# Whole rows for two slabs of W1, the ragged unit and a value tile around the key folds, and the second layer two token tiles ahead, in a gated mix of linear attention and a ReLU layer

## The chip, the cores and the metric

The kernel runs on one core of a Trainium2 chip. The metric is the device time of one execution in microseconds (us). Profiles are of one execution each. TensorE (PE in the profile, PEld for its weight loads), VectorE (DVE), ScalarE (ACT), GpSimd (POOL) and SyncE (SP) run side by side, and each works through its own queue in order. TensorE writes its results into PSUM, which has eight banks of 128 x 512 fp32.

## The reference

The input x has 2048 tokens of width 512. All data are bf16. A linear attention with 32 heads and a two-layer ReLU network read the same x, and a gate per token mixes them:

```python
q, k, v = split(x @ wqkv)                    # 32 heads of 16
pq, pk = q @ w_phi[h], k @ w_phi[h]          # per head, 16 x 16
phi_q = concat(softmax(pq), softmax(-pq))    # 32 features per head
phi_k = concat(softmax(pk), softmax(-pk))
kv, z = phi_k^T v, sum over s of phi_k       # per head
o = (phi_q kv) / (phi_q z + 1e-6)
a = o @ wo
b = relu(x @ w1) @ w2                        # 512 -> 1376 -> 512
g = sigmoid(sum(x * gate_w))
out = g * a + (1 - g) * b
```

## The kernel before

TensorE's work is cut by token tiles of 128 (16 of them, m = 0 to 15) and by chunks of 512 tokens (4 of them, c). The program is written out by hand: each call appends instructions to the queues of the engines, with named events to wait for. The order of the calls is the order on every engine. A list `free` holds, for each PSUM bank, the event that frees it; whoever takes the bank next waits for that event as the list has it at that point of the program.

Loads (L165 to L189) are issued by SP, in this order: the first 512 tokens of x, W1 in slabs of 128 rows (`loadw1`, L161; slab 0 in two pieces, slabs 1 to 3 with the first 1024 of 1376 columns), between slabs 2 and 3 a DMA transpose of part of x (event x0t, L175), then the remaining 352 columns of all four slabs (event w1r, L178), w_phi, the value weights, the query and key weights through two DMA transposes (wqk0, wqk1, L185), and the other three chunks of x through DMA transposes (L188).

Start on TensorE: `slab(t)` (L518) multiplies slab t with the first 512 tokens, for eight blocks of 128 hidden columns, into eight banks. Slab 2 needs x0t. Two more blocks (`hunit(0, 8)` and `hunit(0, 9)`, L269) need all of W1. `hunit(c, k)` computes hidden block k of chunk c with four matmuls, and ScalarE (or VectorE) writes its ReLU to HT. The last 96 hidden columns and the gate's column are the ragged unit `rest(c)` (L279): 16 small matmuls, two activations on ScalarE and a DMA transpose from SP. `pre(i)` (L300) folds w_phi into the query weights (i = 0 to 3, wqk0) and the key weights (i = 4 to 7, wqk1), four matmuls each; the result goes from PSUM to WQK by VectorE (even i) or ScalarE (odd i). `vtile(m)` (L401) computes the values of tile m with four matmuls into bank 2.

Middle: for each tile, `atile(m)` (L319) computes the query and key scores with eight matmuls and starts the softmax chain on ScalarE, VectorE and GpSimd; `kv(m - 3)` (L417) adds the tile's keys and values into banks 6 and 7; then come `vtile(m + 3)` and one to three units of the list `mid` (L563). A pair (c, k) of that list is `hunit(c, k)`, and k = -1 is `rest(c)`. The units left over (`late`, L566) follow, among them the last `kv` calls and `kvfin`, with which VectorE completes the sums. `qchain` (L380) is the query half of the softmax chain; that of tile 15 is called at the end.

Output loop (L608): `nd(m)` (L454) multiplies the query features with the sums (eight short matmuls), VectorE takes the reciprocal (L464) and multiplies (L468), and SP transposes the tile to OT by DMA. `finB(m, bank)` (L479) is the second layer of the ReLU network for a token tile: 11 matmuls into one bank. `finA(m, bank)` (L490) is the output projection: four matmuls, after which ScalarE scales by the gate (L497). `comb(m)` (L502) then adds (1 - g) times the bank of `finB` on VectorE (L506), which frees that bank, and issues the store. `finB` takes the banks of `FB = (4, 5, 7)` by tile modulo 3. In the loop `finB` runs one tile ahead of `finA`. Tile 15 is computed in two column parts in banks 4 and 3 at the end.

Of the kernel before, what the change touches and what calls it, by code (L numbers as in the profile page):

```python
# [68 lines left out]
def bass_gated_mix__linear_kernel_hedgehog__dense_activation_relu__prompt_kernel(  # L69
# [16 lines left out]
    DFF = B_w1.shape[1]  # L86
    P = 128
    NT = S // P
# [13 lines left out]
    KU = KT - 1  # L102
    NR = DFF - KU * P

    with ExitStack() as es:
# [8 lines left out]
        W1 = E(nc.sbuf_tensor("W1", [P, NDT, DFF + 8], BF16))  # L114
# [36 lines left out]
        p = _Plan(["sp", "pool", "act", "dve", "pe"])  # L151
# [9 lines left out]
        def loadw1(t, c0=0, c1=DFF, tag=""):  # L161
            p.dma("sp", lambda e: e.dma_start(  # L162
                out=W1[:, t, c0:c1], in_=B_w1[t * P:(t + 1) * P, c0:c1]), f"w1{t}{tag}", ev=f"w1{t}{tag}")
# [6 lines left out]
        p.early("sp")  # L170
        loadw1(0, 0, 4 * P, "a")
        loadw1(0, 4 * P, 8 * P)
        for t in (1, 2):
            loadw1(t, 0, 8 * P)
        p.dma("sp", lambda e: e.dma_start_transpose(  # L175
            out=XT[:, 2:4, 0:512], in_=x2[0:512, 2 * P:4 * P]), "x0t", ev="x0t")
        loadw1(3, 0, 8 * P)
        p.dma("sp", lambda e: e.dma_start(  # L178
            out=W1[:, :, 8 * P:DFF], in_=B_w1[:, 8 * P:DFF].rearrange("(j p) n -> p j n", p=P)), "w1r", ev="w1r")
        p.dma("sp", lambda e: e.dma_start(  # L180
            out=WPS[:, :, :], in_=A_w_phi.rearrange("(g hl) r c -> (hl r) g c", g=NDT)), "wps", ev="wps")
        p.dma("sp", lambda e: e.dma_start(  # L182
            out=WV[:, :, :], in_=A_wqkv[:, 2 * D:3 * D].rearrange("(j p) n -> p j n", p=P)), "wv", ev="wv")
        for i in range(2):
            p.dma("sp", lambda e, i=i: e.dma_start_transpose(  # L185
                out=WQKT[:, 4 * i:4 * i + 4, :], in_=A_wqkv[:, i * D:(i + 1) * D]), f"wqk{i}", ev=f"wqk{i}")
# [92 lines left out]
        def rest(c):  # L279
            bank = nextbank()  # L280
            for i in range(4):
                for s in range(NDT):
                    t0 = c * 512 + i * P
                    p.op("pe", lambda e, i=i, s=s, t0=t0: e.matmul(  # L284
                        PS[:, bank, i * P:i * P + NR + 1], XT[:, s, t0:t0 + P], W1[:, s, KU * P:DFF + 1],
                        start=(i == 0 and s == 0), stop=(s == NDT - 1), skip_group_check=True),
                        after=(xready(c) + w1all + ["gw"] + free[bank] if i == 0 and s == 0 else ()),
                        ev=(f"h{c}_r" if i == 3 and s == NDT - 1 else None))
            src = PS[:, bank, :].rearrange("p (i n) -> p i n", i=4)
            b = c % 2  # L290
            p.op("act", lambda e: e.activation(HR[:, b, :, 0:NR], src[:, :, 0:NR], ACT.Relu),
                 after=[f"h{c}_r"] + ([f"hr{c - 2}"] if c >= 2 else []), ev=f"rr{c}")
            p.op("act", lambda e: e.activation(
                EG[:, 4 * c:4 * c + 4].unsqueeze(2), src[:, :, NR:NR + 1], ACT.Exp, scale=-1.0), ev=f"eg{c}")
            free[bank] = [f"eg{c}"]
            p.dma("sp", lambda e: e.dma_start_transpose(
                out=HT[:, KU, c * 512:(c + 1) * 512].rearrange("p (i t) -> p i t", i=4),
                in_=HR[:, b, :, :].rearrange("p i n -> p (i n)")), f"hr{c}", after=[f"rr{c}", f"hz{b}"], ev=f"hr{c}")
# [102 lines left out]
        def vtile(m, eng="act", bank=2):  # L401
            b = m % VB
            for dt in range(NDT):
                p.op("pe", lambda e, dt=dt: e.matmul(  # L404
                    PS[:, bank, :], XT[:, dt, m * P:(m + 1) * P], WV[:, dt, :],
                    start=(dt == 0), stop=(dt == NDT - 1)),
                    after=((xready(m // 4) + ["wv"] + free[bank]) if dt == 0 else ()),
                    ev=(f"v{m}" if dt == NDT - 1 else None))
            dst, src = VS[:, b, :, 0:64], PS[:, bank, :].rearrange("p (g c) -> p g c", g=NG)
            after = [f"v{m}"] + ([f"kv{m - VB}"] if m >= VB else [])  # L410
            if eng == "dve":
                p.op("dve", lambda e: e.tensor_copy(dst, src), after=after, ev=f"cv{m}")
            else:
                p.op("act", lambda e: e.activation(dst, src, ACT.Copy), after=after, ev=f"cv{m}")  # L414
            free[bank] = [f"cv{m}"]
# [38 lines left out]
        def nd(m):  # L454
            b0 = 2 * (m % 2)
            after = [f"tq{m}", "kvz0"] + free[b0] + free[b0 + 1]
            for g in range(NG):
                p.op("pe", lambda e, g=g: e.matmul(  # L458
                    PS[:, b0 + g // 4, (g % 4) * GW:(g % 4) * GW + 68],
                    PHQ[:, g, m * P:(m + 1) * P], KVNZ[:, g, :], start=True, stop=True),  # L460
                    after=(after if g == 0 else ["kvz1"] if g == 4 else ()), ev=(f"nd{m}" if g == NG - 1 else None))
            r = m % 2
            ob = m % 3
            p.op("dve", lambda e: e.reciprocal(  # L464
                RDEN[:, r, :].rearrange("p (g h) -> p g h", g=NG),
                bass.AP(tensor=PS, offset=b0 * 512 + 64, ap=[[EPS, P], [GW, NG], [1, HG]])),
                after=[f"nd{m}"], ev=f"rd{m}")
            p.op("dve", lambda e: e.tensor_tensor(  # L468
                OTM[:, ob, :].rearrange("p (g h d) -> p g h d", g=NG, h=HG),
                bass.AP(tensor=PS, offset=b0 * 512, ap=[[EPS, P], [GW, NG], [DH, HG], [1, DH]]),  # L470
                bass.AP(tensor=RDEN, offset=r * H, ap=[[2 * H, P], [HG, NG], [1, HG], [0, DH]]), ALU.mult),
                after=[f"rd{m}"] + ([f"to{m - 3}"] if m >= 3 else []), ev=f"om{m}")
            free[b0] = free[b0 + 1] = [f"om{m}"]
            p.dma("sp", lambda e: e.dma_start_transpose(
                out=OT[:, :, m * P:(m + 1) * P], in_=OTM[:, ob, :]), f"to{ob}", after=[f"om{m}"], ev=f"to{m}")
# [81 lines left out]
        for i in range(4):  # L557
            pre(i)
        vtile(2, "dve")
        for i in range(4, 8):  # L560
            pre(i)
        rest(0)
        mid = [[(1, 0), (1, 1)], [(1, 2), (1, 3)], [(1, 4), (1, 5)], [(1, 6), (1, 7)], [(1, 8), (1, 9)], [(2, 0)],  # L563
               [(1, -1), (2, 1)], [(2, 2), (2, 3)], [(2, 4)], [(2, -1), (2, 5)], [(2, 6), (2, 7)], [(2, 8)],
               [(3, -1), (2, 9)], [(3, 0), (3, 1)], [(3, 2), (3, 3)], []]
        late = [(3, k) for k in range(4, KU)]  # L566

        def unit(c, k):
            if k < 0:
                rest(c)  # L570
            else:
                hunit(c, k)

        for m in range(NT):
            atile(m)
            if m >= LAG:
                kv(m - LAG)
            if m + 3 < NT:
                vtile(m + 3)
            for u in mid[m]:  # L580
                unit(*u)
            if m == 3:
                for a, b in ((0, 5), (5, KU)):
                    p.dma("sp", lambda e, a=a, b=b: e.dma_start(
                        out=W2[:, a:b, :], in_=B_w2[a * P:b * P, :].rearrange("(j p) n -> p j n", p=P)),
                        "w2", ev=f"w2{a}")
                p.dma("sp", lambda e: e.dma_start(out=W2[0:NR, KU, :], in_=B_w2[KU * P:DFF, :]), "w2", ev="w2")
            if m == 5:
                for a in range(0, NDT, 2):
                    p.dma("sp", lambda e, a=a: e.dma_start(  # L590
                        out=WO[:, a:a + 2, :], in_=A_wo[a * P:(a + 2) * P, :].rearrange("(j p) n -> p j n", p=P)),
                        "wo", ev="wo" if a else None)
        for i, u in enumerate(late):
            if i == 0:
                kv(NT - 3)
            if i == 2:
                kv(NT - 2)
            if i == 4:
                kv(NT - 1)
                kvfin()  # L600
            unit(*u)
        nd(0)
        qchain(NT - 1)
        gate()
        finB(0, 4)
        nd(1)
        FB = (4, 5, 7)
        for m in range(NT):  # L608
            if m > 1 and m + 3 < NT:
                nd(m + 3)  # L610
            if m + 1 < NT - 1:
                finB(m + 1, FB[(m + 1) % 3])
            if m == 1:
                nd(m + 3)
            if m == 0:
                nd(2)
                nd(3)
            finA(m, (6, 2, 0)[max(m - NT + 3, 0)])
            if m < NT - 1:
                comb(m)  # L620
        m = NT - 1
# [40 lines left out]
```

## Time and profile before

| what | value |
|---|---|
| median of 3 runs | 147.23 us (146.21 to 147.29) |
| span of the profiled execution, first to last instruction | 146.3 us |
| TensorE busy in 0 to 3.8 us | 3.42 us |
| in 3.8 to 19.3 us | 14.58 us of 15.5 |
| in 19.3 to 88.4 us (tiles) | 69.10 us of 69.1 |
| in 88.4 to 141.8 us (output loop) | 53.40 us of 53.4 |
| in 141.8 to 146.3 us | 2.54 us of 4.5 |
| granted TensorE clock, all stages | 1.000 |

The profile page gives the busy time of each engine and the chain of work that ended last, followed back from the last instruction; a line such as L483 is that of the function that issued the instruction. The list of waits says which engine waited for whom: total us, number of times, longest. The chain in order of time and the timeline have a start, a duration, an engine, a line and an operation with a count; in the timeline a bracket holds the idle time before a group, and what ended it. Matmuls are pipelined: one with 512 columns has a row of 0.38 us, but they start every 0.216 us, and the chain counts them by that distance.

### The profile page before, as it was taken

To read this page: it belongs to the slowest core of one execution; us is meant where nothing else is said; L and a number is where in the kernel's file an instruction comes from. 1 tells how busy PE (TensorE), PEld (TensorE's weight loads), DVE (VectorE), ACT (ScalarE), POOL (GpSimd) and SP (SyncE) were. 2 spreads that over 40 slices of the span, in tenths; PEclk is the share of its full clock that TensorE was granted. 3 is DMA by queue.
4 is the path that set the end of the run, shared out by engine and by line. 5 is a ranking of instruction groups with operands and counts; after the bars stand their busy time and mean duration, and the time that the engine had idled before them with its cause. 6 is when DMAs were issued, how large, how long until landed. Compare 5 with 4: busy or idle time off the path is not lost.

```text
span 146.3 us, 2520 instructions
## 1 busy us (share of the span) xinstructions
PE 143.0 (98%) x970; PEld 72.3 (49%) x970; DVE 91.7 (63%) x156; ACT 72.4 (49%) x124; POOL 52.2 (36%) x62
## 2 busy tenths in 40 slices
PE   8999799999999999999999999999999999999994
PEld 3444564444455545544645555554444444444443
DVE  4338627777687878678698977674445555555342
ACT  4134467798778778887878862022221111111150
POOL 2013002778768678688869820300000000000000
DMA  5998998033549984335333431354333223222213
GB/s 150 262 276 163 231 167 186 3 69 72 76 80 328 179 201 73 72 72 108 78 72 75 104 72 31 81 108 117 85 82 78 72 72 76 72 72 74 72 44 106
DMA packets 46517, 16.12 MB, mean 110 GB/s; under 512 B 40392, under 2 KB 46120, under 8 KB 46504
## 3 DMA queue, kind: packets, MB, share of 16 engines
q1 hardware_dynamic: 46352, 15.92, 50.3%
q8 instruction: 8, 0.13, 0.4%
q10 hardware_dynamic: 152, 0.03, 0.1%
q14 instruction: 5, 0.04, 0.1%
HBM read 4.15 MB, written 2.10 MB: 43 GB/s over the span
## 4 chain that ended last, share of the span: by engine, by line
PE 86%; SPq 7%; DMA 4%; DVE 1%; issue 0%
PE PS L483 26%; PE PS L328 18%; PE PS L272 18%; PE PS L492 9%; PE PS L404 8%; SPq L185 4%; DMA PHQ<-in_A_wqkv_dram 4%; PE PS L458 3%; PE PS L426 3%; PE PS L284 2%; SPq L162 2%; SPq L175 1%; PE PS L306 1%; DVE WQK L506 1%; SPq L182 0%
## 5 line engine op out<-in xcount | busy, mean ns | idle before, releaser
L483 PE MATMUL PS<-W,HT 128*128 128x512 bf16 (+4 forms) x187 | 40.6, 366 | 0.0
L372 POOL TENSOR_TENSOR EB<-EB,SC 128x1024 bf16<-128x1024 bf16 x15 | 28.9, 1930 | 23.4 <-DVE SC L370 23.4
L348 ACT ACTIVATE EB<-PS 128x480 bf16<-128x480 f32 (+1 forms) x44 | 30.1, 756 | 14.2 <-PE PS L328 14.2
L497 ACT ACTIVATE TFA<-PS,GT 128x512 bf16<-128x512 f32 x16 | 11.0, 687 | 42.7 <-PE PS L492 36.6
L272 PE MATMUL PS<-XT,W 128*128 128x512 bf16 x128 | 30.7, 379 | 0.0
L328 PE MATMUL PS<-WQK,XT 128*128 128x480 bf16 x128 | 28.5, 366 | 0.0
L368 DVE TENSOR_REDUCE ZB<-EB 128x64 f32<-128x1024 bf16 x15 | 18.3, 1220 | 14.7 <-ACT EB L348 14.7
L506 DVE SCALAR_TENSOR_TENSOR WQK<-PS,OMG,TFA 128x512 bf16<-128x512 f32 (+2 forms) x17 | 12.2, 719 | 23.6 <-ACT TFA L497 22.4
L483 PEld LDWEIGHTS PS<-W,HT 128*128 128x128 bf16 (+1 forms) x187 | 17.0, 98 | 17.4
L258 ACT ACTIVATE HT<-PS 128x512 bf16<-128x512 f32 x35 | 20.3, 614 | 7.4 <-PE PS L520 5.6
L328 PEld LDWEIGHTS PS<-WQK,XT 128*128 128x128 bf16 x128 | 12.5, 98 | 13.6
L383 DVE TENSOR_REDUCE ZB<-EB 128x64 f32<-128x1024 bf16 x16 | 18.6, 1164 | 0.0
L272 PEld LDWEIGHTS PS<-XT,W 128*128 128x128 bf16 x128 | 12.0, 98 | 13.2
L392 POOL TENSOR_TENSOR EB<-EB,SC 128x512 bf16<-128x512 bf16 x16 | 16.9, 1059 | 1.3
L404 PE MATMUL PS<-WV,XT 128*128 128x512 bf16 x64 | 16.2, 378 | 0.0
L492 PE MATMUL PS<-WO,OT 128*128 128x512 bf16 x64 | 16.1, 378 | 0.0
L468 DVE TENSOR_TENSOR WQK<-PS,RDEN 128x512 bf16<-128x512 f32 x16 | 11.1, 692 | 0.5
L492 PEld LDWEIGHTS PS<-WO,OT 128*128 128x128 bf16 x64 | 6.1, 97 | 7.2
L414 ACT ACTIVATE VS<-PS 128x512 bf16<-128x512 f32 x14 | 8.5, 608 | 2.0 <-PE PS L404 2.0
L370 DVE RECIPROCAL SC<-ZB 128x64 f32<-128x64 f32 x16 | 8.8, 553 | 0.5
L458 PEld LDWEIGHTS PS<-KVNZ,PHQ 128*128 128x128 bf16 x128 | 6.1, 97 | 3.6
L404 PEld LDWEIGHTS PS<-WV,XT 128*128 128x128 bf16 x64 | 5.4, 97 | 4.8
(57 smaller groups left out, 85.7 us busy)
## 6 DMA issues: line engine op xcount, KB each, us to landing
out_dram<-WQK SPq DMA_DIRECT2D x15, 128.0 KB, 1.7
W<-in_B_w_dram SPq DMA_DIRECT2D x2, 640.0 KB, 5.8
W<-in_B_w_dram SPq DMA_DIRECT2D x3, 256.0 KB, 3.8
WV<-in_A_wqkv_dram SPq DMA_DIRECT2D x1, 512.0 KB, 6.5
WO<-in_A_wo_dram SPq DMA_DIRECT2D x2, 256.0 KB, 3.0
W<-in_B_w_dram SPq DMA_DIRECT2D x1, 352.0 KB, 5.1
OT<-in_A_x_dram SPq DMA_DIRECT2D x2, 128.0 KB, 2.3
W<-in_B_w_dram SPq DMA_DIRECT2D x2, 128.0 KB, 3.0
```

Of the source, the lines that this page charges most:

```text
L258: p.op("act", lambda e: e.activation(dst, src, ACT.Relu), after=[f"h{c}_{kt}"], ev=ev)
L272: p.op("pe", lambda e, t=t: e.matmul(PS[:, bank, :], W1[:, t, kt * P:(kt + 1) * P], XT[:, t, c * 512:(c + 1) * 512], start=(t == 0), stop= ...
L328: p.op("pe", lambda e, dt=dt, which=which: e.matmul(PS[:, which, 0:DE], XT[:, dt, m * P:(m + 1) * P], WQK[:, which, dt * DE:(dt + 1) * DE] ...
L348: p.op("act", lambda e: e.activation(dst, s_, ACT.Exp, scale=scale), after=[f"qk{m}"] + busy, ev=ev)
L368: p.op("dve", lambda e: e.tensor_reduce(zk, ek, AX.X, ALU.add), after=[emk, f"cst{b}"], ev=f"zk{m}")
L372: p.op("pool" if m < NT - 1 else "dve", lambda e: e.tensor_tensor(EB[:, b, 3, :].rearrange("p (g f) -> p g f", f=DH), EB[:, b, 2, :].rearr ...
L383: p.op("dve", lambda e: e.tensor_reduce(ZB[:, b, 0:64].rearrange("p (h s) -> p h s", s=2), bass.AP(tensor=EB, offset=base, ap=[[EBS, P], [ ...
L392: p.op("pool", lambda e: e.tensor_tensor(EB[:, b, 0, :].rearrange("p (h s f) -> p h s f", h=H, s=2)[:, :, 1, :], EB[:, b, 1, :].rearrange( ...
L404: p.op("pe", lambda e, dt=dt: e.matmul(PS[:, bank, :], XT[:, dt, m * P:(m + 1) * P], WV[:, dt, :], start=(dt == 0), stop=(dt == NDT - 1)), ...
L483: p.op("pe", lambda e, kt=kt, M=M: e.matmul(PS[:, bank, 0:n], HT[0:M, kt, m * P:(m + 1) * P], W2[0:M, kt, cs], start=(kt == 0), stop=(kt = ...
L492: p.op("pe", lambda e, t=t: e.matmul(PS[:, bank, :], OT[:, t, m * P:(m + 1) * P], WO[:, t, :], start=(t == 0), stop=(t == NDT - 1)), after ...
L506: p.op("dve", lambda e: e.scalar_tensor_tensor(out=OSB[:, ob, cs], in0=PS[:, bank, 0:n], scalar=OMG[:, m:m + 1], in1=TFA[:, m % 2, cs], op ...
```

## The change

Slabs 2 and 3 of W1 are loaded with all their 1376 columns, and the transfer of the remaining columns covers slabs 0 and 1 only. `rest(0)` moves ahead of `pre(4)` to `pre(7)`, and `vtile(3)` moves from the first pass of the tile loop to the place behind `pre(7)`. The units of `mid` move one place forward, so that `late` holds five units in place of six. In the output part `finB` runs two tiles ahead of `finA`: `finB(0)` comes ahead of `nd(0)`, and the loop calls `finB(m + 2)`. The three banks of `FB` stay. The bank of `finA` for the last three tiles is 2, 0 and 6 in place of 6, 2 and 0.

```diff
--- before.py
+++ after.py
@@ -170,13 +170,14 @@
         p.early("sp")
         loadw1(0, 0, 4 * P, "a")
         loadw1(0, 4 * P, 8 * P)
-        for t in (1, 2):
-            loadw1(t, 0, 8 * P)
+        loadw1(1, 0, 8 * P)
+        loadw1(2)
         p.dma("sp", lambda e: e.dma_start_transpose(
             out=XT[:, 2:4, 0:512], in_=x2[0:512, 2 * P:4 * P]), "x0t", ev="x0t")
-        loadw1(3, 0, 8 * P)
+        loadw1(3)
         p.dma("sp", lambda e: e.dma_start(
-            out=W1[:, :, 8 * P:DFF], in_=B_w1[:, 8 * P:DFF].rearrange("(j p) n -> p j n", p=P)), "w1r", ev="w1r")
+            out=W1[:, 0:2, 8 * P:DFF], in_=B_w1[0:2 * P, 8 * P:DFF].rearrange("(j p) n -> p j n", p=P)),
+            "w1r", ev="w1r")
         p.dma("sp", lambda e: e.dma_start(
             out=WPS[:, :, :], in_=A_w_phi.rearrange("(g hl) r c -> (hl r) g c", g=NDT)), "wps", ev="wps")
         p.dma("sp", lambda e: e.dma_start(
@@ -557,13 +558,14 @@
         for i in range(4):
             pre(i)
         vtile(2, "dve")
+        rest(0)
         for i in range(4, 8):
             pre(i)
-        rest(0)
-        mid = [[(1, 0), (1, 1)], [(1, 2), (1, 3)], [(1, 4), (1, 5)], [(1, 6), (1, 7)], [(1, 8), (1, 9)], [(2, 0)],
-               [(1, -1), (2, 1)], [(2, 2), (2, 3)], [(2, 4)], [(2, -1), (2, 5)], [(2, 6), (2, 7)], [(2, 8)],
-               [(3, -1), (2, 9)], [(3, 0), (3, 1)], [(3, 2), (3, 3)], []]
-        late = [(3, k) for k in range(4, KU)]
+        vtile(3)
+        mid = [[(1, 0), (1, 1), (1, 2)], [(1, 3), (1, 4)], [(1, 5), (1, 6)], [(1, 7), (1, 8)], [(1, 9), (2, 0)], [(2, 1)],
+               [(1, -1), (2, 2)], [(2, 3), (2, 4)], [(2, 5)], [(2, -1), (2, 6)], [(2, 7), (2, 8)], [(2, 9)],
+               [(3, -1), (3, 0)], [(3, 1), (3, 2)], [(3, 3), (3, 4)], []]
+        late = [(3, k) for k in range(5, KU)]
 
         def unit(c, k):
             if k < 0:
@@ -575,7 +577,7 @@
             atile(m)
             if m >= LAG:
                 kv(m - LAG)
-            if m + 3 < NT:
+            if 0 < m and m + 3 < NT:
                 vtile(m + 3)
             for u in mid[m]:
                 unit(*u)
@@ -599,23 +601,24 @@
                 kv(NT - 1)
                 kvfin()
             unit(*u)
+        FB = (4, 5, 7)
+        finB(0, FB[0])
         nd(0)
         qchain(NT - 1)
         gate()
-        finB(0, 4)
+        finB(1, FB[1])
         nd(1)
-        FB = (4, 5, 7)
         for m in range(NT):
             if m > 1 and m + 3 < NT:
                 nd(m + 3)
-            if m + 1 < NT - 1:
-                finB(m + 1, FB[(m + 1) % 3])
+            if m + 2 < NT - 1:
+                finB(m + 2, FB[(m + 2) % 3])
             if m == 1:
                 nd(m + 3)
             if m == 0:
                 nd(2)
                 nd(3)
-            finA(m, (6, 2, 0)[max(m - NT + 3, 0)])
+            finA(m, (6, 2, 0, 6)[max(m - NT + 4, 0)])
             if m < NT - 1:
                 comb(m)
         m = NT - 1
```

## The prediction

> **What bounds the kernel now.** I read the page first: how busy each engine is, and which chain ended last.
>
> ```profile
> span 146.3 us, 2520 instructions
> PE 143.0 (98%) x970; PEld 72.3 (49%) x970; DVE 91.7 (63%) x156; ACT 72.4 (49%) x124; POOL 52.2 (36%) x62
> ...
> PE 86%; SPq 7%; DMA 4%; DVE 1%; issue 0%
> ```
>
> TensorE is busy for 98% and carries 86% of the chain; the rest is the start (SP's queue and a DMA) and a short tail. An edit can save only TensorE's few idle moments, but can lose any amount by making it wait. The list of TensorE's waits shows what is to be had:
>
> ```profile
> PE PS L306 <- DMA PHQ<-in_A_wqkv_dram: 0.9, 2, 0.5
> ```
>
> Two waits of the key folds (pre, L306), 0.9 us together. Next, the first stage of the chain in order of time:
>
> ```profile
> 12.41 5.12 DMA PHQ<-in_A_wqkv_dram
> 17.53 0.04 issue
> 17.57 1.01 PE PS L306 x16
> 18.59 0.69 PE PS L284 x16
> 19.28 1.62 PE PS L328 x8
> ```
>
> The second transposed load lands at 17.53; folds 4 to 7 wait for it, and the ragged unit (rest, L284) comes behind them. From here to 141.9 the chain lies on TensorE without a break. Last, one period of the output loop in the timeline (start, duration, engine, line):
>
> ```profile
> 104.46 1.03 PE L492 MATMUL PS<-WO,OT 128*128 128x512 bf16 x4
> ...
> 105.33 0.42 PE L458 MATMUL PS<-KVNZ,PHQ 128*128 128x68 bf16 x8
> 105.53 0.69 ACT L497 ACTIVATE TFA<-PS,GT 128x512 bf16<-128x512 f32 x1 [2.81 <-PE PS L492]
> ...
> 105.58 2.54 PE L483 MATMUL PS<-W,HT 128*128 128x512 bf16 x11
> 106.25 0.75 DVE L506 SCALAR_TENSOR_TENSOR WQK<-PS,OMG,TFA 128x512 bf16<-128x512 f32 x1 [1.76 <-ACT TFA L497]
> 106.92 0.35 DVE L464 RECIPROCAL RDEN<-PS 128x32 f32<-128x32 f32 x1
> ```
>
> finA(m-1) ends at 105.49, ScalarE scales it from 105.53 to 106.22, VectorE combines (comb) from 106.25 to 107.00. Meanwhile TensorE has long begun the next finB (105.58), in a bank that an older tile freed. In the chain this period is nd 0.26 + finB 2.38 + finA 0.86 = 3.50 us, all TensorE.
>
> **Second layer two tiles ahead: a new wait.** finB uses three banks, FB = (4, 5, 7), by tile mod 3. Before, finB(m+1) takes the bank of tile m-2, combined a whole period ago. After, finB(m+2) takes the bank of tile m-1, and is issued right behind finA(m-1), with only nd(m+3) between. A bank is freed by comb, and comb(m-1) needs finA(m-1) and its scaling first. So TensorE must wait for the scaling and the combination of the tile it has just finished, in each of the iterations m = 1 to 12 (finB(3) to finB(14)). Queued behind the waiting matmul are finA(m) and all that follows on TensorE; VectorE and ScalarE only feed that same chain.
>
> The new period, from finA's first matmul to the next finA's: finA 1.03 (timeline) + 0.04 until ScalarE starts + 0.69 + 0.03 + combination 0.75 + release of TensorE by VectorE + finB 2.38. No row of this loop shows that release. Nearest: VectorE's memset of ONE ends at 0.32 and the first weight load starts at 0.38 (0.06), and in the first slab, released by a DMA, the matmul starts 0.03 behind its weight load (3.78, 3.81). I take 0.09. Bounds: VectorE's next instruction starts 0.08 before the combination's end (106.92 against 107.00), so the release may come that early; and a queued weight load leads its matmul by 0.22 (97.00, 97.22), so 0.28. Sum: 1.03 + 0.04 + 0.69 + 0.03 + 0.75 + 0.09 + 2.38 = 5.01, against 3.50. nd(m+3), 0.26, falls inside the wait.
>
> The first pass differs: nd(2) and nd(3) stand together before finA(0), so VectorE's reciprocals and multiplications of both delay comb(0). In the trace finA(0) ends at 95.00 and comb(0) at 95.91 + 0.74 = 96.65, 1.65 later. nd(4) comes behind finB(3) and is not covered. From finA(0) to finA(1): 1.02 + 1.65 + 0.09 + 2.38 + 0.25 = 5.39.
>
> From finA(0) to finA(12): 5.39 + 11 x 5.01 = 60.50, before 135.93 - 93.98 = 41.95: **+18.55**. finB(14) now precedes finA(12), so from there to finA(13) 0.86 instead of 3.24 (139.17 - 135.93): -2.38. finB(2) stands before finA(0) instead: +2.38. The transposes of the attention tiles still come in time: of nd(15) the reciprocal and multiplication end about 1.05 behind the wait, the transpose takes 2.4 to land, 3.5 in all, and finA(15) begins 2.38 + 3 x 0.86 = 4.96 behind it. The tail from finA(13) on stays at 7.1 us; its banks 2, 0 and 6 were freed earlier.
>
> **finB(0) before nd(0), one late unit fewer:** nd(0) has no idle before it in the trace (kvfin ends at 87.60, nd(0) starts at 88.20), so more cover is worth 0. The fifteenth tile's query chain (qchain) and the gate on VectorE move later by one finB; their users are nd(15) and the first scaling, far behind. 0.
>
> **Ragged unit and value tile 3 around the folds.** vtile(2)'s four matmuls start at 16.15 and take 4 x 0.216, so TensorE could go on at 17.01; folds 4 to 7 start at 17.57: 0.56 lost. rest(0) (0.69) there ends at 17.70, past the landing at 17.53, so the wait is covered: **-0.56**. Value tile 3 (0.86) then stands where rest stood, covering the evictions of the last folds; atile(0) asks for query weights first and for the key weights 0.8 later. ScalarE gets rest's two activations (0.49 and 0.17) ahead of the evictions of folds 5 and 7 (0.52 each): rest's data at about 17.9, last eviction about 19.6, atile(0) needs it at 17.70 + 1.01 + 0.86 + 0.81 = 20.4. If that cover were gone, ScalarE's lateness would come in whole. rest's DMA transpose now has its data earlier, but SP is busy with the x loads until 22.33 and still issues it then: 0. Moving each projection unit one place forward leaves the sum of matmuls the same; x chunk 1 lands at 19.4 (14.70 + 4.7), before its first use at 21.2.
>
> **Whole rows for slabs 2 and 3.** Same bytes, same number of issues on SP (0.43 us each). Ahead of the x0t transpose go 96 KB more, ahead of slab 3's end 192 KB. At 258 to 327 GB/s (windows from 4 to 5 us and 16 to 17 us) that is 0.3 to 0.4 and 0.6 to 0.7 us. x0t landed at 7.43 (3.03 + 4.4), and slab 2's matmuls start at 11.14 - 16 x 0.216 = 7.69; slab 3 landed at 8.21 and is needed at 9.41. So TensorE may lose 0.1 to 0.2 at slab 2, nothing at slab 3. TensorE's idle time ahead of the first folds (0.52, waiting for a transpose at 15.30) takes that up: 0. Without that cover it costs that 0.2. The remainder w1r has half its short rows and lands no later than its 10.13, before 10.9. The folds' transposes have the same bytes ahead. Bounds of the whole front: -1.1 (both waits gone) to +0.3 (transposes late).
>
> **The sum:** 18.55 - 0.56 = +18.0. The span 146.3 becomes 164.3; the median of the runs is 147.23, 0.9 above the profiled span, so **165.2 us**.
>
> **Rivals.** *The bank wait is covered* (the side of not slower): if the combination of tile m-1 were done before finB(m+2) is at the head, only the front's gain is left, 147.2 - 0.6 = 146.7. It decides at scaling plus combination, 1.6 us behind finA's end, against the 0.26 of nd that stands between: six times too little cover. A fourth bank would be needed, and FB has three. Chance 0.04.
>
> *The clock falls.* With 1.3 us idle in each 5, TensorE might be slowed. Row first: in windows of 1 us with TensorE busy for 0.70 and 0.60 (15 to 16, 17 to 18) the granted clock stays 1.000. The trace's first matmuls do show another pitch, weight loads at 0.78, 1.21, 1.64, 0.43 apart against 0.216. By 0.43: finA 3 x 0.43 + 0.63 = 1.92, the chain 1.60, finB 11 x 0.43 = 4.73, period 8.25; 11 x (8.25 - 3.50) and the first give about 55 more: 202. Half as much if it swings. Against it: no wait of over 2 us. Chance 0.05.
>
> The Trainium skill, "TensorE: Matmul & The Clock Gate", section "A second HAM failure mode: psum-queue depth-cycling", speaks for this rival: a kernel that cycled banks paused often enough for its clock to swing between half and full. Its table of the two states asks for an idle window of some 3.4 us before the clock halves. By the first the sum would be about 200, by the second it stays; no run shown here has such pauses.
>
> *The waits come, but at another size* is inside the forecast.
>
> **How the numbers follow.** Forecast 0.88, the two rivals 0.09, others 0.03 (a smaller loss, near 155). Twelve waits by the release's bounds: 12 x (-0.17) = -2.0 to 12 x 0.19 = +2.3; with the front 162.6 to 168.4 at the ends. Both ends at once are unlikely: 163.2 to 167.6 holds 0.8. A measurement tells 1% from no change: slower 0.96, same 0.03, faster 0.01.
>
> **What would show it.** On TensorE's list of waits: finB (L483) released by VectorE's L506, 12 times, about 1.3 each and 1.7 for the first, some 16 us. Period 5.0 in the loop, TensorE busy at 87%, L497 and L506 in the chain with about 5% each. L306's second wait gone, the output loop's finA(0) at 93.98 - 0.56 + 2.38 = 95.8. Wrong if the period stays 3.5, or if matmuls in the loop stand 0.43 apart.

## The result and the profile after

| | before | after |
|---|---|---|
| median of 4 runs | 147.24 us (146.21 to 147.29) | 165.07 us (164.55 to 165.5) |
| span of the profiled execution | 146.3 us | 163.9 us |
| ratio of the times | | 1.1246, 95% interval 1.1198 to 1.1293 |

The change makes the kernel slower by 17.8 us; 165.2 had been forecast. The four runs of before scatter by 1.1 us; against the 55 later ones, with medians of 146.65 to 146.79 us, the loss is 18.3 to 18.4 us. The page of the changed kernel, with the parts that were read of before (the line numbers of the functions are one higher than before: L484 is `finB`, L493 `finA`, L498 the scaling, L507 the combination):

```profile
span 163.9 us, 2508 instructions
PE 145.0 (88%) x970; PEld 72.8 (44%) x970; DVE 91.8 (56%) x156; ACT 72.2 (44%) x124; POOL 52.1 (32%) x62
...
PE 84%; DVE 7%; ACT 5%; DMA 2%; issue 1%; SPq 0%
```

TensorE's busy time is the same within 2 us, but the span has grown by 17.6, and ScalarE and VectorE have entered the chain that ended last. TensorE's list of waits (total, times, longest):

```profile
PE PS L484 <- DVE WQK L507: 16.4, 12, 1.7
```

Twelve waits of finB for the combination, and none is left for the key folds. One period of the loop in the timeline:

```profile
105.92 1.03 PE L493 MATMUL PS<-WO,OT 128*128 128x512 bf16 x4
...
106.79 0.42 PE L459 MATMUL PS<-KVNZ,PHQ 128*128 128x68 bf16 x8
106.99 0.69 ACT L498 ACTIVATE TFA<-PS,GT 128x512 bf16<-128x512 f32 x1 [4.37 <-PE PS L493]
107.71 0.75 DVE L507 SCALAR_TENSOR_TENSOR WQK<-PS,OMG,TFA 128x512 bf16<-128x512 f32 x1 [3.32 <-ACT TFA L498]
...
108.52 2.55 PE L484 MATMUL PS<-W,HT 128*128 128x512 bf16 x11 [1.31 <-DVE WQK L507]
```

The projection of a tile ends at 106.95, the scaling runs to 107.68, the combination to 108.46, and only then does the next finB start, after 1.31 us in which TensorE does nothing. In the profile of before finB started at 105.58, when the scaling had just begun (105.53), and ahead of the combination (106.25).

### The profile page after: what moved, and what is told of

It reads as the page before. It is cut to its first block, busy times and chain, and to the rows that moved or that the text cites. A ratio compares the mean times of both kernels' runs of the same rounds, so it can differ in the third digit from the quotient of the medians.

```text
span 163.9 us, 2508 instructions
## 1 busy us (share of the span) xinstructions
PE 145.0 (88%) x970; PEld 72.8 (44%) x970; DVE 91.8 (56%) x156; ACT 72.2 (44%) x124; POOL 52.1 (32%) x62
## 4 chain that ended last, share of the span: by engine, by line
PE 84%; DVE 7%; ACT 5%; DMA 2%; issue 1%; SPq 0%
PE PS L484 24%; PE PS L273 17%; PE PS L329 16%; PE PS L405 8%; PE PS L493 8%; DVE WQK L507 6%; ACT TFA L498 5%; PE PS L521 5%; PE PS L427 2%; PE PS L285 2%; DMA OT<-in_A_x_dram 2%; PE PS L307 1%; PE PS L459 1%; DVE WQK L469 0%; DVE RDEN L465 0%
## 5 line engine op out<-in xcount | busy, mean ns | idle before, releaser
L484 PE MATMUL PS<-W,HT 128*128 128x512 bf16 (+4 forms) x187 | 40.7, 367 | 16.4 <-DVE WQK L507 16.4
L498 ACT ACTIVATE TFA<-PS,GT 128x512 bf16<-128x512 f32 x16 | 11.0, 687 | 61.1 <-PE PS L493 52.7
L507 DVE SCALAR_TENSOR_TENSOR WQK<-PS,OMG,TFA 128x512 bf16<-128x512 f32 (+2 forms) x17 | 12.2, 719 | 37.8 <-ACT TFA L498 36.6
L484 PEld LDWEIGHTS PS<-W,HT 128*128 128x128 bf16 (+1 forms) x187 | 16.8, 98 | 35.3 <-DVE WQK L507 13.7
L273 PE MATMUL PS<-XT,W 128*128 128x512 bf16 x128 | 30.7, 379 | 0.0
L369 DVE TENSOR_REDUCE ZB<-EB 128x64 f32<-128x1024 bf16 x15 | 18.3, 1220 | 14.8 <-ACT EB L349 14.8
L493 PE MATMUL PS<-WO,OT 128*128 128x512 bf16 x64 | 15.9, 378 | 0.0
L465 DVE RECIPROCAL RDEN<-PS 128x32 f32<-128x32 f32 x16 | 5.6, 350 | 6.6 <-PE PS L459 6.6
L493 PEld LDWEIGHTS PS<-WO,OT 128*128 128x128 bf16 x64 | 6.1, 97 | 7.2
L521 PE MATMUL PS<-XT,W 128*128 128x512 bf16 x32 | 7.7, 392 | 0.0
```

Of the source, the lines that this page charges most:

```text
L273: p.op("pe", lambda e, t=t: e.matmul(PS[:, bank, :], W1[:, t, kt * P:(kt + 1) * P], XT[:, t, c * 512:(c + 1) * 512], start=(t == 0), stop= ...
L369: p.op("dve", lambda e: e.tensor_reduce(zk, ek, AX.X, ALU.add), after=[emk, f"cst{b}"], ev=f"zk{m}")
L484: p.op("pe", lambda e, kt=kt, M=M: e.matmul(PS[:, bank, 0:n], HT[0:M, kt, m * P:(m + 1) * P], W2[0:M, kt, cs], start=(kt == 0), stop=(kt = ...
L493: p.op("pe", lambda e, t=t: e.matmul(PS[:, bank, :], OT[:, t, m * P:(m + 1) * P], WO[:, t, :], start=(t == 0), stop=(t == NDT - 1)), after ...
L498: p.op("act", lambda e: e.activation(TFA[:, m % 2, :], PS[:, bank, :], ACT.Copy, scale=GT[:, m:m + 1]), after=[f"fa{m}", "gt"] + ([f"cb{m ...
L507: p.op("dve", lambda e: e.scalar_tensor_tensor(out=OSB[:, ob, cs], in0=PS[:, bank, 0:n], scalar=OMG[:, m:m + 1], in1=TFA[:, m % 2, cs], op ...
```

## The experiments

All edits are against the changed kernel or against the kernel before, as each says. The ratios are to runs of the kernel before on the same chip: 146.65 us (median of 17) for the output part, the start, four banks and two banks; 146.79 (29) for the scaling twice, the bank freed early, the loads and the moves; 146.73 (9) for the quarter of the scaling, the scaling twice one ahead, and the kernel before again.

**The output part alone.** The kernel before, with the new order and banks of the output loop and nothing else:

```diff
+        FB = (4, 5, 7)
+        finB(0, FB[0])
         nd(0)
...
-            if m + 1 < NT - 1:
-                finB(m + 1, FB[(m + 1) % 3])
+            if m + 2 < NT - 1:
+                finB(m + 2, FB[(m + 2) % 3])
```

> The kernel before with the output part of the change alone. Theory (the bank wait): the period of the output loop is 5.00 us as in the changed kernel, and the total is that of before plus the 18.5 us that the waits cost, 165.7 us; TensorE waits 12 times for the combination on VectorE, 16 us in all. Rival (part of the loss comes from the moved loads and units at the start): less, 150 to 163 us.

Measured: 165.41 us, ratio 1.1272 (1.1242 to 1.1302), 18.8 us more, with 12 waits of 16.4 us in all, as in the changed kernel. The whole loss is in this part.

**The start alone.** The new loads, folds and units, with the output part of before:

> The changed kernel's loads, folds and units with the output part of before. Theory: the first stages win what the trace of the changed kernel shows, 0.87 us, so 146.4 us, and the loop's period is 3.50 us. Rival (the start is no gain, its delay of 0.4 us at the first slab eats it): 147.2 us or more.

Measured: 147.02 us, ratio 1.0015 (0.9997 to 1.0032). No gain; the theory's 0.87 us is not there. The period is 3.50 us again. The last four experiments below look for the reason.

**Four banks.** The changed kernel with a fourth bank for finB:

```diff
-            b0 = 2 * (m % 2)
+            b0 = 0
...
-        FB = (4, 5, 7)
+        FB = (4, 5, 7, 3)
...
-                finB(m + 2, FB[(m + 2) % 3])
+                finB(m + 2, FB[(m + 2) % 4])
```

> The changed kernel, two tiles ahead, but with four banks for the second layer; the fourth comes from nd, which uses one pair of banks for all tiles. Theory (bank distance): finB(m + 2) finds the bank of tile m - 2, free for a period; period 3.50 us, no wait behind the combination; nd(3) waits once for nd(2)'s bank, some 1.1 us: 147.5 us. Rival (running two tiles ahead costs by itself, by the later projection or the transposes): about 165 us.

Measured: 148.09 and 148.64 us in two runs at a granted clock of 1.000, ratio 1.0109 (1.0069 to 1.0149); two more took 150.80 and 150.88 us, at a mean granted clock of 0.998 and 0.994. From the chain of the first, start, duration, engine and line:

```profile
101.61 2.38 PE PS L484 x11
103.98 0.87 PE PS L493 x4
104.85 0.26 PE PS L459 x8
105.10 2.38 PE PS L484 x11
```

Two tiles ahead, and the period is 3.50 us: the lead itself costs nothing. The two waits that this kernel has are those of nd for its single pair of banks (1.7 us, about what the first two runs take longer than before; two in place of the one that was expected, since nd(5) comes soon behind nd(4) as nd(3) behind nd(2)). The profile is of the run of 148.09; what the two longer runs lost stays open.

**Two banks, one ahead.** The kernel before with a bank less:

```diff
-        FB = (4, 5, 7)
+        FB = (4, 5)
...
-                finB(m + 1, FB[(m + 1) % 3])
+                finB(m + 1, FB[(m + 1) % 2])
...
-            finB(m, (4, 3)[i], cs, "ab"[i])
+            finB(m, (7, 3)[i], cs, "ab"[i])
```

> The kernel before, one tile ahead, with two banks for the second layer instead of three (the last tile's first part moves to bank 7). Theory (bank distance): finB(m + 1) waits for the combination of tile m - 1 in 13 iterations, period 5.00 us, 147.2 + 20.2 = 167.4 us. Rival (it is the lead of two tiles that costs): 147.2 us.

Measured: 166.88 us, ratio 1.1363 (1.1328 to 1.1397). From its list of waits:

```profile
PE PS L483 <- DVE WQK L506: 18.0, 13, 1.7
```

The old order, with a lead of one, makes the same wait, once per tile. Lead and banks count only together: with one bank more than the lead, finB takes the bank of the tile whose projection has just ended.

**The scaling twice.** To see whether ScalarE's step stands in what TensorE waits for, the changed kernel issues it twice, the second waiting for the first:

```diff
-            p.op("act", lambda e: e.activation(
-                TFA[:, m % 2, :], PS[:, bank, :], ACT.Copy, scale=GT[:, m:m + 1]),
-                after=[f"fa{m}", "gt"] + ([f"cb{m - 2}"] if m >= 2 else []), ev=f"ta{m}")
+            for i in range(2):
+                p.op("act", lambda e: e.activation(
+                    TFA[:, m % 2, :], PS[:, bank, :], ACT.Copy, scale=GT[:, m:m + 1]),
+                    after=([f"fa{m}", "gt"] + ([f"cb{m - 2}"] if m >= 2 else [])) if i == 0 else [f"tx{m}"],
+                    ev=f"ta{m}" if i else f"tx{m}")
```

> The changed kernel with ScalarE's scaling of the output projection issued twice. Theory (ScalarE's step stands in the chain that TensorE waits for): each of the 12 waits grows by the second activation, 0.6 to 0.7 us, 165.1 + 8 = 173 us. Rival (the wait is set by something else, VectorE's own turn or SP): 165 us.

Measured: 186.72 us, ratio 1.2721 (1.2693 to 1.2749): 14 us more than the theory says. Its waits:

```profile
PE PS L484 <- DVE WQK L509: 24.9, 12, 2.3
```

24.9 less 16.4 is 8.5 us, the 8 that was expected. The rest is not waiting. Windows from one finB to the next (window, length, busy us of PE, PEld, DVE, ACT and POOL, granted clock, DMA), and weight loads from the first slow one:

```profile
104.80:110.50 5.70, 3.65 (x23) 1.77 (x23) 1.63 (x4) 1.37 (x2) 0.00 (x0) 1.00 0.19 46
110.50:117.90 7.40, 5.35 (x23) 2.21 (x23) 1.73 (x4) 1.37 (x2) 0.00 (x0) 0.77 0.17 38
117.90:125.30 7.40, 5.37 (x24) 2.18 (x25) 1.72 (x4) 1.37 (x2) 0.00 (x0) 0.77 0.14 35
125.30:131.10 5.80, 3.68 (x24) 1.80 (x25) 1.81 (x4) 1.37 (x2) 0.00 (x0) 1.00 0.18 45
```

```profile
112.20 0.15 PEld L484 LDWEIGHTS PS<-W,HT 128*128 128x128 bf16 x1 [0.28 <-issue]
112.63 0.15 PEld L484 LDWEIGHTS PS<-W,HT 128*128 128x128 bf16 x1 [0.27 <-issue]
113.06 0.15 PEld L484 LDWEIGHTS PS<-W,HT 128*128 128x128 bf16 x1 [0.28 <-issue]
```

From the third of the 12 waits on (finB(5), at 110.5), in two periods of three, the matmuls stand 0.43 us apart for a while, as in the first microseconds of every trace here, and the mean granted clock of such a period is 0.77. This is the rival of the falling clock, which the changed kernel with its pauses of 1.3 us does not show (1.000 in all four runs).

**A quarter of the scaling again,** to see where between the two the clock gives way: the second activation is for 128 columns.

> The changed kernel with the scaling issued a second time for a quarter of the columns, so that TensorE's pause grows from 1.3 to about 1.6 us, between the changed kernel and the one with the scaling twice (2.0 us, where the clock fell). If the pause alone adds, 12 x 0.3: 168.7 us and clock 1.000. Rival (the clock falls here already): over 172 us and a mean clock under 1.

Measured: 170.15 us at clock 1.000 in the profiled run, and 171.65 at 0.990 in the other. The profiled run waits 21.1 us in all, 1.76 for each, where about 1.6 had been expected; its span of 168.9 is 5.0 more than that of the changed kernel, and its waits are longer by 4.7. With these pauses the pause alone adds in one execution, and the clock begins to fall in another.

**The scaling twice, one ahead.** The same doubling in the kernel before:

> The kernel before, one tile ahead with three banks, with the scaling issued twice. Theory (there the bank's release is covered by a whole period): no wait in the loop, only the tail's last scalings come later, 147.2 to 148 us. Rival (ScalarE's step is on the path in any order): 155 us.

Measured: 147.27 us, ratio 1.0025 (1.0000 to 1.0051). Sixteen more activations of 0.69 us cost 0.4 us, at most 0.75, where they cost 8.5 us of waiting (and the clock) two tiles ahead. The three banks are the same; what differs in the loop is the lead, and with it how soon a bank is taken again.

**The bank freed early.** The changed kernel, three banks and two ahead, but ScalarE empties finB's bank as soon as it is complete, and VectorE adds in SBUF:

```diff
+        def early(m):
+            bank = fbank[(m, "")]
+            p.op("act", lambda e: e.activation(
+                OSB[:, m % 3, :], PS[:, bank, :], ACT.Copy, scale=OMG[:, m:m + 1]),
+                after=[f"fb{m}", "gt"] + ([f"out{m - 3}"] if m >= 3 else []), ev=f"tb{m}")
+            free[bank] = [f"tb{m}"]
...
             if m > 1 and m + 3 < NT:
                 nd(m + 3)
+            if m + 1 < NT - 1:
+                early(m + 1)
```

> The changed kernel, two tiles ahead with three banks, but the bank of the second layer is emptied by ScalarE (scaled by 1 - g into the output tile) as soon as finB is done, and the combination adds in SBUF. Theory: the bank is free before the projection of its tile begins, no wait, period 3.50 us, 146.4 us, as the front alone. Rival (the lead itself or the third bank costs): 165 us, or something between if ScalarE, now with two activations of 0.69 us in 3.5, comes late.

Measured: 146.85 us, ratio 1.0008 (0.9987 to 1.0028). No wait of TensorE in the loop is left. From its timeline:

```profile
107.28 2.54 PE L484 MATMUL PS<-W,HT 128*128 128x512 bf16 x11
107.81 0.68 ACT L505 ACTIVATE WQK<-PS,OMG 128x512 bf16<-128x512 f32 x1
107.94 0.42 DVE L512 TENSOR_TENSOR WQK<-WQK,TFA 128x512 bf16<-128x512 bf16 x1 [2.08 <-ACT TFA L498]
```

The same lead and the same three banks: what makes the loss is that the release hangs on the projection.

**The loads alone and the moves alone.** The kernel before with the new loads of W1, and the kernel before with `rest(0)`, `vtile(3)` and the units moved:

> The kernel before with whole rows for slabs 2 and 3 alone. Theory (fewer short rows ahead of the transposes): the first slab's second half lands at 5.3 in place of 5.0 us, but the query and key weights' transposes land 0.7 us or more earlier, as in the trace of the changed kernel (key weights before 17 us): 146.7 us. Rival (both shifts are scatter from run to run): the key weights at 17.5 us, 147.2 us.

> The kernel before with the ragged unit ahead of folds 4 to 7 and value tile 3 behind them, with the old loads. Theory: the wait ahead of folds 4 to 7 is covered, 0.56 us, the one ahead of folds 0 to 3 stays: 146.7 us. Rival (the gain needs the new loads): 147.2 us.

Measured: 146.68 us, ratio 0.9993 (0.9981 to 1.0006), and 146.83 us, 0.9999 (0.9983 to 1.0016). Neither changes the time. But the moves have a loss of their own in these two kernels, in the start alone and in the moves alone: with one late unit fewer and no finB ahead of it, nd(0) comes so soon that its fifth matmul waits for the last step of kvfin (L439). From the timeline of the moves alone:

```profile
87.67 0.62 PE L458 MATMUL PS<-KVNZ,PHQ 128*128 128x68 bf16 x8
87.77 0.17 DVE L439 SCALAR_TENSOR_TENSOR KVNZ<-PS,M 128x16 bf16<-128x16 f32 x1
...
87.99 0.18 PEld L458 LDWEIGHTS PS<-KVNZ,PHQ 128*128 128x128 bf16 x4 [0.15 <-DVE KVNZ L439]
```

These eight matmuls have a row of 0.42 us in before and in the changed kernel, where finB(0) stands ahead of nd(0). So 0.2 us of loss hides in the two medians.

The loads do shift the transposes. The issue of the query weights' transpose, us to landing, in the first profile of before (issued at 6.60):

```profile
PHQ<-in_A_wqkv_dram SPq DMA_TRANSPOSE x1, 8.7
```

and with the new loads alone (issued at 6.64):

```profile
PHQ<-in_A_wqkv_dram SPq DMA_TRANSPOSE x1, 6.9
```

It lands at 15.3 and at 13.5. In seven profiles with the old loads it landed between 14.4 and 15.3, in seven with the new ones between 13.5 and 13.9. That is no scatter, yet the median shows no gain (at most 0.3 us by the interval).

**The kernel before, twice more,** to see why not:

> The kernel before, unchanged, profiled once more. Theory (the waits of the folds in the first profile were at the long end of a scatter): with a span of about 145.4 us, the key weights land before 17.2 us and TensorE waits less than 0.9 us for both transposes. Rival (the waits are the same in every execution): 0.9 us again, and the key weights at 17.5 us.

> The same, a second time: a further sample of the landing times, of the wait ahead of the folds and of the moment from which the first slab's matmuls start 0.216 us apart.

Spans of 145.6 and 145.7 us, and the theory held: the key weights land at 16.8 and 16.6 us, and in both TensorE's list has no wait for the transposes. (In the first of them the weight loads of folds 4 to 7 wait 0.46 us, of which some 0.14 reach the chain.) The weight loads of the first slab in the second of them, and then the second group of folds (L306):

```profile
5.46 0.15 PEld L520 LDWEIGHTS PS<-XT,W 128*128 128x128 bf16 x1 [0.28 <-issue]
5.89 5.56 PEld L520 LDWEIGHTS PS<-XT,W 128*128 128x128 bf16 x26 [0.28 <-issue]
...
16.75 1.05 PEld L306 LDWEIGHTS PS<-Wbd,PHQ 128*128 128x128 bf16 x16
```

Here the matmuls stand 0.43 us apart until 5.9; in the first profile of before they did so until 5.0. The slabs end later for it, by 0.4 and 0.6 us, and the query weights land at 14.5 and 14.4 in place of 15.3: both make TensorE come to the folds when the transposes have landed, and the wait is gone without any change. By the chains, atile(0) begins at 18.57 and 18.66 in these two and at 19.28 in the first profile; in the three other profiles with the old start at 18.58, 18.77 and 19.15. In the six profiles with the new start, less the 0.86 for the value tile that they have done by then, it is 17.77 to 18.71. The means are 18.84 and 18.41, so the profiles hint at a gain of 0.4 us from loads and moves together, not clear of their scatter of 0.7 and 0.9. The times allow less: the bank freed early, which has the new start and no wait at nd(0), gains at most 0.2 us by its interval.

No version beats the kernel before: the new loads alone, at 146.68, are level with it.

## Why the prediction was right

**The bank wait** was right in place, count and size. Forecast were 12 waits, 1.7 us for the first and 1.3 for the others, 16 in all; the trace has 12, 1.71 and 1.31 to 1.40, 16.4 in all. The distance from finA(0) to finA(12) was put at 60.50 us and is 60.41 (first matmuls at 95.49 and 155.90). The release of TensorE, taken as 0.09 between bounds of -0.08 and 0.28, shows as 0.05 in most periods and 0.14 in some. The output part alone costs 18.8 us between medians, forecast 18.55. Four banks, two banks in the old order, and the early release show that the bank is the cause, not the lead; the scaling doubled in both orders shows that ScalarE's step is in the chain only where the bank is reused too soon.

**finB(0) ahead of nd(0), one late unit fewer, and the tail,** put at 0, were right in the changed kernel: the chain has no wait at nd(0), and from finA(13) on it takes 7.1 us as before. But the step priced only the added cover. The unit taken from `late` costs 0.2 us by itself, as the start alone and the moves alone show; finB(0) covers it.

**The front, -0.56 us, was wrong in size.** The step read one wait ahead of folds 4 to 7 from one execution as if it stood in all of them. In the pair of first profiles the start did gain, 0.87 us (finA(0) at 95.49, against 93.98 + 2.38 = 96.36), but between medians the moves alone give 0.0 with an interval of about 0.25 us to each side, and of the six profiles with the old start three have a wait for the transposes on TensorE's list (0.9, 0.6 and 0.3 us) and three have none. Without the 0.2 us at nd(0), which the changed kernel does not pay, the moves alone would gain some 0.2 us by estimate. What took its place is scatter on both sides of the wait. The first slab's matmuls are slow for a time that differs from run to run, so that in the profiles the weight loads behind the slabs begin anywhere between 10.7 and 11.6; and with the old loads the query weights land anywhere between 14.4 and 15.3. The first profile of before had an early TensorE (10.9) and the latest landing.

**The loads, 0,** were right in time and wrong in one reason: the transposes do not land as before. The query weights' transpose came 0.5 to 1.8 us earlier with half the short rows ahead of it, and the weights of the values too (4.9 to 5.2 us from issue to landing in place of 5.6 to 6.5). That TensorE waits for them only in some executions is a likely reason why this shows in no median. The working also had the bytes wrong: the 352 moved columns of a slab are 88 KB, not 96, and of two slabs 176, not 192, which hardly moves the delays that it estimates. The transpose x0t took 4.3 to 5.0 us to land with the new loads and 4.1 to 4.5 with the old, so it came later about as estimated.

**The sum** came nearer than its terms. The base of 147.23 us, a median of three runs, was 0.5 us above the medians of the later runs, and the -0.56 of the front, most of which did not come, took that back: here the forecast had luck.

**The rivals.** The covered wait did not come, as its own condition said; with a fourth bank TensorE does not wait for the combination. The falling clock did not come at 1.3 us. It came at 2.1, near where the step "no wait of over 2 us" had drawn the line by chance: of the two rules quoted there from the Trainium skill ("TensorE: Matmul & The Clock Gate"), the section on the second failure mode is borne out by the doubled scaling (granted clock 0.77 in two periods of three), and the idle window of some 3.4 us in the table of the two states is not needed for it: no pause of that kernel is longer than 2.3 us.

## What to carry to other kernels

A stage that runs k tiles ahead through n buffers takes, for its next tile, the buffer of the tile n - k behind the one now being consumed: with n = k + 1 it waits for the consumer that stands just ahead of it in its own queue, and pays on each tile for as much of that consumer's chain as no other work covers (here 1.3 us of 1.6). Either a buffer more, or a release that doesn't hang on the late operand, makes the lead free; here it then bought nothing, since TensorE had no gap to fill in this loop. A wait of half a microsecond that one execution shows behind a load wants a second profile before it is counted as a gain. And a part of a change, taken alone, can lose cover that another part gave it.

## What the runs showed of the hardware

TensorE's granted clock held at 1.000 with a pause of 1.3 us in every 5.0 us, was 1.000 in one run and 0.990 in another with 1.76 us, and with 2.07 us in every 5.7 it was 0.77 in two periods of three (which grew to 7.4 us), 0.935 over the whole run. With the same doubled scaling and no pauses, one tile ahead, it stayed at 0.998 or more in all eight runs. The cost jumped with it: 8.5 us more of waiting became 21.7 us more of time.

At the start of every profile matmuls of 512 columns stood 0.43 us apart, at a granted clock that the profile gives as 1.00, and the change to 0.216 came anywhere from under 4 to 6.2 us (at about 5.0, 5.7 and 5.9 in the three profiles of the kernel before). And with 256 rows of 704 bytes fewer ahead of it, their bytes loaded in longer rows of other transfers, a DMA transpose landed about 1 us earlier (13.5 to 13.9 us against 14.4 to 15.3); that it is the number of rows, and not the order of the bytes, was not tested apart.
